# Chunked scan feeding a gated feed-forward: two constant tables filled by VectorE, the first two up-projection units taken by channel half, and one weight product placed behind pair 1's output

## The chip, the cores and the metric

The kernel runs on one core of one Trainium2 chip. The metric is the device time of one execution in microseconds. Each kernel's time is a median over several executions; the profile is of one further execution, whose own time is given beside its span. Engines: PE (TensorE matmul; PEld is its weight load), DVE (VectorE), ACT (ScalarE), POOL (GpSimd), SP (SyncE, which here only issues transfers).

## The reference

Two stages follow each other. The first is a chunked linear recurrence per batch (4) and head (8) over a sequence of 768, with head width D = 32 and state width N = 16; the second multiplies two projections of its result and projects back.

```python
# x (4,8,768,32)  a (4,8,768)  B, C (4,8,768,16)
for c in range(nc):
    cum = cumsum(log a within the chunk)
    L = exp(cum_i - cum_j) * (i >= j)                    # causal
    y_intra = ((C @ B^T) * L) @ x
    y_inter = (C @ state) * exp(cum)
    y = y_intra + y_inter
    state = decay_full * state + sum_j B_j x_j decay_from_j
X = y.transpose(0, 2, 1, 3).reshape(3072, 256)
out = ((X @ w_a) * (X @ w_b)) @ w_out                    # w_a, w_b (256,1536), w_out (1536,256)
```

The output is (3072, 256) in float32.

## The kernel before

The sequence is cut into 6 blocks of 128 tokens. A *pair* is two batches of one block, so there are 12 pairs (pair p is block p // 2). Pairs 0 to 3 go through the feed-forward one pair at a time, in half-precision operands with float32 sums; later blocks go through it a whole block at a time.

For one pair the steps are these. The decays within a block are a product scan on DVE (`scan`, line 227, into `Pr`); B and C are scaled by its quotients (`scale_bc`), turned by PE (`transposes`), and evacuated to `bt` (ACT) and `ct` (DVE). `scores` (line 373) makes C·Bᵀ for all heads in four PSUM banks, `SC[0]` to `SC[3]`; `mask` multiplies each of the four by the table `causal`. Three of the four are done by DVE straight out of PSUM (line 413). The fourth is copied to SBUF by ACT (`tmp`, line 410) and multiplied by POOL (line 411). `scale_x` (line 287, ACT) makes the half-precision `X16` from the loaded `xn`. `pv` multiplies the masked scores with `X16` (line 433), makes the state's terms (line 460), and evacuates the pair's output to `X2T` in two parts, one on ACT (line 492) and one on DVE (line 493). For pair 0 the output is made in two *channel halves* u = 0, 1: `pv_u(0, 0)`, `pv_u(0, 1)`, each followed by two evacuations (`evac0`).

The feed-forward of a pair has 6 *units* k2, each 256 of the 1536 hidden columns. `unit_mm(p, k2, W)` (line 601) is four matmuls of 128x256: two column groups kk, and for each the two channel halves f = 0, 1 that are summed in one PSUM bank. With `Wa` it makes `aps`, which ACT copies to SBUF as `asb` (`evac_a`, line 615); with `Wb` it makes `bps`; DVE multiplies the two into `hk` (`times`, line 622). The output product (line 637) runs over `hk` later.

The order of all work is written out by hand (`manual_schedule`): each engine runs its instructions in the order of the program text, and semaphores carry the dependences between engines. The order around the change is this: pair 0 to its output; `transposes(1)`; units (0,0) and (0,1) with `Wa`; `hr`, `hs`, `hsx` on POOL (three small products, of which `gps` is made); `scores(1)`; the fourth mask of pair 1; unit (0,2) with `Wa`; `factors`; `scale_x(1)`; the three other masks; units (0,0), (0,1), (0,2) with `Wb`; the first `times`; `pv(1)`; the state terms of pair 0; `gps` (line 810) and its copy `G`; the other two `times`; units (1,0), (1,1), (1,2).

PSUM banks for the feed-forward come from `bank(name)` (line 127): four banks, 0 to 3, handed out in the order of the calls by the string `BANKS`. Its first digits are 0 1 2 3 1 0 2 3 1 0 2 3 1 0 1 2 3 0 1; the calls they answer are `fps`, `tb`, `tc`, `py0`, `py1`, three `aps` of pair 0, `fps` of `factors`, three `bps` of pair 0, `gps`, and then `aps` and `bps` of (1,0), of (1,1) and of (1,2). A matmul that starts a new use of a bank waits until the engine that reads the bank's previous content has finished.

Transfers are issued by three engines. SP and ACT issue those of pair 0 at the start. POOL, after it has made its tables `sel`, `ident` and `causal`, issues the rest of pair 1's B and C, the first halves of `Wa` and `Wb`, and pair 1's `xn`; the loads on POOL's queue follow the tables in the order of the text (lines 211 to 216).

Of the kernel before, what the change touches and what calls it, by code (L numbers as in the profile page):

```python
# [28 lines left out]
def kernel(  # L29
# [13 lines left out]
    nc = tc.nc  # L43
# [3 lines left out]
    Q = 128  # L47
# [27 lines left out]
    ident = const.tile([128, 128], f16, name="ident")  # L75
    causal = const.tile([128, 2, Q], f16, name="causal")
# [10 lines left out]
    Wa = [big.tile([128, 2, KC], f16, name=f"Wa{t}") for t in range(2)]  # L87
    Wb = [big.tile([128, 2, KC], f16, name=f"Wb{t}") for t in range(2)]
    Wo = big.tile([128, NK, d_model], f16, name="Wo")
    X2T = big.tile([128, P0, 2, 2, Q], f16, name="X2T")  # L90
# [36 lines left out]
    def bank(name):  # L127
        return psf.tile([128, 512], f32, name=name, tag=f"ff{next(banks)}")
# [58 lines left out]
    load1(nc.sync, 1, 0, 0)  # L187
    nc.sync.dma_start(c32, p32_t.ap())
    nc.vector.memset(warm.bitcast(u32), 0)
    nc.vector.memset(zero, 0.0)  # L190
    nc.gpsimd.memset(sel, 1.0)
    nc.gpsimd.affine_select(
# [5 lines left out]
        pattern=[[-H, 2], [-2 * H, NBP], [-1, H]],  # L198
        channel_multiplier=1,
    )  # L200
    nc.gpsimd.memset(ident, 1.0)
    nc.gpsimd.affine_select(
        out=ident, in_=ident, compare_op=ALU.is_equal, fill=0.0, base=0, pattern=[[-1, 128]], channel_multiplier=1
    )
    nc.gpsimd.memset(causal, 1.0)
    for bt in range(2):
        v = causal[64 * bt : 64 * bt + 64]
        nc.gpsimd.affine_select(  # L208
# [23 lines left out]
    def sel_over_mid(lo, hi, eng):  # L232
        eng.tensor_tensor(
            out=selr[:, lo:hi].rearrange("p k t c -> p k (t c)"),
            in0=sel.rearrange("p t b h -> p (t b h)").unsqueeze(1).broadcast_to((BH, hi - lo, 2 * NBP * H)),
            in1=rmid[:, lo:hi].unsqueeze(2).broadcast_to((BH, hi - lo, 2 * NBP * H)),
            op=ALU.mult,
        )
# [113 lines left out]
    def scores(p):  # L352
        BT, CT = st[p]["BT"], st[p]["CT"]
        st[p]["T1"] = mid.tile([128, H, 2, Q], f16, name="t1", tag="t1")
        for e, bt, m in itertools.product(range(2), range(2), range(4)) if p >= P0 else ():
            rows = slice(32 * m, 32 * m + 32)
            c0 = (e * 2 + bt) * Q
            nc.tensor.matmul(  # L358
                SC[m][:, c0 : c0 + Q],
                BT[rows, e, bt],  # L360
                CT[rows, bt],
                start=True,
                stop=True,
                skip_group_check=True,
                tile_position=(32 * m, 0),
            )
        for e in range(2) if p < P0 else ():
            for r in range(2):
                for m in range(4):
                    for bt in range(2):  # L370
                        rows = slice(32 * m, 32 * m + 32)
                        c0 = (e * 2 + r) * Q
                        nc.tensor.matmul(  # L373
                            SC[m][64 * bt : 64 * bt + 64, c0 : c0 + Q],
                            BT[rows, e, r, bt],
                            CT[rows, bt],
                            start=True,
                            stop=True,
                            skip_group_check=True,
                            tile_position=(32 * m, 64 * bt),  # L380
                        )

    def product(p, m):

        if p >= P0:
            return (
                st[p]["T1"][:, 2 * m : 2 * m + 2].rearrange("p e t q -> p (e t) q"),
                SC[m].rearrange("p (c q) -> p c q", q=Q),
            )
        return (  # L390
            st[p]["T1"][:, 2 * m : 2 * m + 2].rearrange("p e r q -> p e (r q)"),
            SC[m].rearrange("p (e c) -> p e c", e=2),
        )
# [8 lines left out]
    def mask(out_in, by_pool=False, by_token=False):  # L402
        o_, i_ = out_in
        if by_token:
            c_ = causal_q.unsqueeze(1).broadcast_to((128, 4, Q))
        else:
            c_ = causal.rearrange("p r q -> p (r q)").unsqueeze(1).broadcast_to((128, 2, 2 * Q))
        if by_pool:
            tmp = mid.tile([128, *c_.shape[1:]], f32, name="tmp", tag="tmp")
            nc.scalar.copy(tmp, i_)  # L410
            nc.gpsimd.tensor_tensor(out=o_, in0=tmp, in1=c_, op=ALU.mult)  # L411
        else:
            nc.vector.tensor_tensor(out=o_, in0=i_, in1=c_, op=ALU.mult)  # L413
# [182 lines left out]
    def unit_mm(p, k2, W):  # L596
        ps = bank("aps" if W is Wa else "bps")
        for kk in range(2):
            k = 2 * k2 + kk
            for f in range(2):  # L600
                nc.tensor.matmul(  # L601
                    ps[:, kk * 2 * Q : (kk + 1) * 2 * Q],
                    W[k // 6][:, f, k % 6 // 3 * 384 : (k % 6 // 3 + 1) * 384].rearrange("p (c kk) -> p kk c", kk=3)[
                        :, k % 3
                    ],
                    X2T[:, p, :, f],
                    start=(f == 0),
                    stop=(f == 1),
                    skip_group_check=True,
                )  # L610
        return ps

    def evac_a(a_ps, on_dve=False):
        asb = ffh.tile([128, 512], f32, name="asb", tag="asb")
        (nc.vector.tensor_copy if on_dve else nc.scalar.copy)(asb, a_ps)  # L615
        return asb

    def times(p, k2, b_ps, asb):
        s = st[p]
        if "hk" not in s:  # L620
            s["hk"] = ffh.tile([128, NK, 2 * Q], f16, name="hk", tag="hk")
        nc.vector.tensor_tensor(  # L622
            out=s["hk"][:, 2 * k2 : 2 * k2 + 2, :].rearrange("p k q -> p (k q)"), in0=b_ps, in1=asb, op=ALU.mult
        )

    def unit(p, k2, between=None):
        a_ps = unit_mm(p, k2, Wa)
        if between:
            between()
        b_ps = unit_mm(p, k2, Wb)  # L630
        asb = evac_a(a_ps)
        return lambda: times(p, k2, b_ps, asb)
# [26 lines left out]
    def bunit(blk, k):  # L659
        s = st.setdefault(("FF", blk), {})  # L660
        if "hk" not in s:
            s["hk"] = hkb.tile([128, NK, 2 * NBP * Q], f16, name="hkb", tag="hkb")
        ps = []
        for W in (Wa, Wb):
            t_ = bank("aps" if W is Wa else "bps")
            for f in range(2):
                nc.tensor.matmul(  # L667
                    t_,
                    W[k // 6][:, f, k % 6 // 3 * 384 : (k % 6 // 3 + 1) * 384].rearrange("p (c kk) -> p kk c", kk=3)[
                        :, k % 3  # L670
                    ],
                    XB[:, blk - P0 // NBP, f].rearrange("p t j q -> p (t j q)"),
                    start=(f == 0),
                    stop=(f == 1),
                    skip_group_check=True,
                )
            ps.append(t_)
        asb = evac_a(ps[0])
        return lambda: nc.vector.tensor_tensor(out=s["hk"][:, k], in0=ps[1], in1=asb, op=ALU.mult)  # L679
# [93 lines left out]
    scan(5, NBLK)  # L773
    over_mid(1, NBLK)
    sel_over_mid(1, NBLK, nc.vector)
    aps = [unit_mm(0, 0, Wa), unit_mm(0, 1, Wa)]
    asb = [evac_a(aps[0])]
    nc.gpsimd.tensor_tensor(out=hr, in0=Pr[:, 0:NG, Q - 1], in1=rmid[:, 0:NG], op=ALU.mult)
    nc.gpsimd.tensor_tensor(out=hs, in0=hr, in1=Pr[:, 1:NBLK, 63], op=ALU.mult)
    nc.gpsimd.tensor_tensor(  # L780
# [2 lines left out]
        in1=selb.rearrange("p (b g) -> p b g", b=nb),  # L783
        op=ALU.mult,
    )
    scores(1)
    mask(product(1, 3), by_pool=True)
    aps.append(unit_mm(0, 2, Wa))
    asb.append(evac_a(aps[1]))
    asb.append(evac_a(aps[2]))  # L790
# [2 lines left out]
    scale_x(1, nc.scalar)  # L793
    for m in range(3):
        mask(product(1, m))
    bps = [unit_mm(0, k2, Wb) for k2 in range(3)]
    for bt in range(2):
        load1(nc.gpsimd, 2, 1, bt)
    load_wo(0)
# [9 lines left out]
    for c0 in (0, 64):  # L809
# [4 lines left out]
            start=True,  # L814
            stop=True,
            skip_group_check=True,
            tile_position=(0, c0),
        )
    nc.scalar.copy(G.rearrange("p b g -> p (b g)"), gps[:, 0 : nb * NG])
    for k2 in range(1, 3):  # L820
        times(0, k2, bps[k2], asb[k2])
    fb(1)
# [233 lines left out]
```

## Time and profile before

| | us |
|---|---|
| median of 3 runs | 123.72 |
| the runs | 122.92, 124.85, 123.72 |
| the profiled execution | 122.51 |
| span of its profile | 120.8 |
| PE busy | 115.7 (96% of the span) |
| DVE, ACT, POOL busy | 85.2, 72.1, 62.3 |
| first feed-forward matmul, from the span's start | 10.58 |

The profiled execution's own time is 1.71 us longer than its span, and the kernel's time is this sum, not the span alone. Times in the trace count from the span's start. In the chain of waits each piece has its start, its length, its engine, what it writes and its line; in the chain PE's pieces are put by the ends of their matmuls, so a piece starts where the one before it ended. In the timeline each row has start, length, engine, line, operation, output and inputs, count, and in square brackets the idle time ahead of it with what ended it; there a matmul's length holds its whole passage, 0.27 us for one of 128x256, while a new one starts every 0.11 us.

### The profile page before, as it was taken

The page shows a single profiled execution, that of the slowest core. Times are in us where ns is not written, and L with a number is a line of the kernel's source. Part 1 is how long each engine was busy: PE and PEld are TensorE (multiplying, and loading weights), DVE is VectorE, ACT ScalarE, POOL GpSimd, SP SyncE. Part 2 cuts the span into 40 slices and gives each one's busy share as a digit, 9 for nine tenths or more (in the row PEclk, how much of TensorE's full clock was granted, in tenths as well). Part 3 has the DMA queues.
Part 4 walks back from the last instruction along what each step waited for, and adds up shares of the span by engine and source line. Part 5 has one row for each costly group of instructions (what it writes and reads, how often), then busy time and mean ns, then how long its engine had stood idle before and what let it go on. Part 6 is the DMA issues. An engine that isn't in the chain of part 4 may idle for free.

```text
span 120.8 us, 3711 instructions
## 1 busy us (share of the span) xinstructions
PE 115.7 (96%) x1455; PEld 79.4 (66%) x1455; DVE 85.2 (71%) x162; ACT 72.1 (60%) x142; POOL 62.3 (52%) x108
## 2 busy tenths in 40 slices
PE   5889999999999999999999999999999999999990
PEld 2445889888898898644476464766464684555890
DVE  1887888882989898499984999677799445847100
ACT  0466757854965767877668637645646737566220
POOL 7999998972795676299731993138400000000200
PEclk9999999999999999999999999999999999999999
DMA  3999999986969999699998874869501012010032
GB/s 62 171 169 233 173 201 159 215 140 70 100 99 126 128 125 144 111 135 146 71 151 111 173 239 126 91 90 159 180 3 49 0 43 87 0 49 0 20 110 87
DMA packets 66641, 13.73 MB, mean 114 GB/s; under 512 B 61616, under 2 KB 66256, under 8 KB 66624
## 3 DMA queue, kind: packets, MB, share of 16 engines
q1 hardware_dynamic: 62448, 9.40, 50.7%
q0 software_dynamic: 2176, 3.74, 17.0%
q10 hardware_dynamic: 2000, 0.36, 1.6%
q8 instruction: 11, 0.18, 0.7%
q14 instruction: 6, 0.05, 0.1%
HBM read 11.13 MB, written 3.15 MB: 118 GB/s over the span
## 4 chain that ended last, share of the span: by engine, by line
PE 89%; DMA 4%; POOL 3%; issue 0%; ACT 0%; POOLq 0%
PE ops L694 18%; PE aps L667 18%; PE bps L667 17%; PE ops L637 9%; PE aps L601 9%; PE bps L601 9%; DMA Wa<-in_moe_w_a_dram 4%; PE SC L358 2%; PE SC L419 2%; POOL cn L148 1%; PE SC L373 1%; PE SC L433 1%; PE SC L508 1%; POOL bn L148 1%; POOL causal L208 1%; PE SC L460 1%
## 5 line engine op out<-in xcount | busy, mean ns | idle before, releaser
L615 ACT COPY asb<-aps 128x512 f32<-128x512 f32 x72 | 41.8, 586 | 14.1 <-PE aps L667 9.7
L679 DVE TENSOR_TENSOR hkb<-bps,asb 128x512 f16<-128x512 f32 x48 | 32.3, 687 | 12.8 <-ACT asb L615 11.6
L667 PE MATMUL aps<-XB,Wa 128*128 128x512 f16 x96 | 28.6, 379 | 0.0
L667 PE MATMUL bps<-XB,Wb 128*128 128x512 f16 x96 | 28.5, 379 | 0.0
L694 PE MATMUL ops<-Wo,hkb 128*128 128x256 f16 (+1 forms) x204 | 22.5, 267 | 0.0
L694 PEld LDWEIGHTS <-hkb 128*128 128x128 f16 x204 | 18.5, 98 | 3.1
L413 DVE TENSOR_TENSOR t<-SC,causal_q 128x512 f16<-128x512 f32 x27 | 17.1, 681 | 3.3 <-PE SC L358 3.3
L622 DVE TENSOR_TENSOR hk<-bps,asb 128x512 f16<-128x512 f32 x24 | 16.2, 685 | 2.4 <-ACT asb L615 1.2
L667 PEld LDWEIGHTS <-Wb 128*128 128x128 f16 x96 | 9.9, 103 | 10.9
L667 PEld LDWEIGHTS <-Wa 128*128 128x128 f16 x96 | 9.7, 103 | 9.1 <-issue 0.2
L708 POOL DMA_DIRECT2D out_dram<-osb x1 | 0.6, 639 | 27.3 <-ACT osb L706 27.3
L706 ACT ACTIVATE osb<-ops 128x256 f32<-128x256 f32 (+1 forms) x16 | 6.0, 376 | 14.3 <-PE ops L694 14.2
L601 PE MATMUL aps<-X2T,Wa 128*128 128x256 f16 x96 | 14.0, 273 | 0.1
L601 PE MATMUL bps<-X2T,Wb 128*128 128x256 f16 x96 | 13.8, 273 | 0.0
L637 PE MATMUL ops<-Wo,hk 128*128 128x256 f16 x96 | 11.5, 273 | 0.0
L601 PEld LDWEIGHTS <-Wa 128*128 128x128 f16 x96 | 9.5, 104 | 1.1 <-DMA Wa<-in_moe_w_a_dram 0.3
L601 PEld LDWEIGHTS <-Wb 128*128 128x128 f16 x96 | 9.8, 103 | 0.6
L411 POOL TENSOR_TENSOR t<-tmp,causal_q 128x512 f16<-128x512 f32 x5 | 5.8, 1159 | 8.0 <-ACT tmp L410 7.9
L637 PEld LDWEIGHTS <-hk 128*128 128x128 f16 x96 | 8.9, 98 | 1.4
L304 POOL TENSOR_TENSOR bm<-bn,fB 128x256 f16<-128x256 f32 x11 | 7.1, 641 | 4.8 <-DMA bn<-in_B_dram 3.6
L289 POOL TENSOR_SCALAR x<-xn 128x512 f16<-128x512 f32 x6 | 8.9, 1489 | 1.0 <-DMA xn<-in_x_dram 0.7
L296 POOL TENSOR_TENSOR planes<-cn,fC 128x256 f16<-128x256 f32 x8 | 5.0, 621 | 7.9 <-DMA cn<-in_C_dram 7.8
(95 smaller groups left out, 124.0 us busy)
## 6 DMA issues: line engine op xcount, KB each, us to landing
out_dram<-osb SPq DMA_DIRECT2D x22, 128.0 KB, 1.8
xn<-in_x_dram SPq DMA_DIRECT2D x7, 256.0 KB, 4.3
cn<-in_C_dram SPq DMA_DIRECT2D x8, 128.0 KB, 4.1
bn<-in_B_dram SPq DMA_DIRECT2D x8, 128.0 KB, 4.6
Wa<-in_moe_w_a_dram POOLq DMA_DIRECT2D x2, 384.0 KB, 5.9
Wb<-in_moe_w_b_dram POOLq DMA_DIRECT2D x2, 384.0 KB, 7.3
Wo<-in_moe_w_out_dram POOLq DMA_DIRECT2D x2, 384.0 KB, 7.2
xn<-in_x_dram POOLq DMA_DIRECT2D x4, 128.0 KB, 7.2
```

What stands on the lines that cost most here:

```text
L289: eng.tensor_scalar(xo, xi, XS, None, ALU.mult)
L304: eng.tensor_tensor(out=m_, in0=raw, in1=(f[:, blk, :, bp] if factor is None else factor).unsqueeze(3).broadcast_to((128, 2, H, N)), op=AL ...
L411: nc.gpsimd.tensor_tensor(out=o_, in0=tmp, in1=c_, op=ALU.mult)
L413: nc.vector.tensor_tensor(out=o_, in0=i_, in1=c_, op=ALU.mult)
L601: nc.tensor.matmul(ps[:, kk * 2 * Q : (kk + 1) * 2 * Q], W[k // 6][:, f, k % 6 // 3 * 384 : (k % 6 // 3 + 1) * 384].rearrange("p (c kk) -> ...
L615: (nc.vector.tensor_copy if on_dve else nc.scalar.copy)(asb, a_ps)
L622: nc.vector.tensor_tensor(out=s["hk"][:, 2 * k2 : 2 * k2 + 2, :].rearrange("p k q -> p (k q)"), in0=b_ps, in1=asb, op=ALU.mult)
L637: nc.tensor.matmul(o_ps[:, 0:d_model], hk[:, k, bt * Q : (bt + 1) * Q], Wo[:, k, :], start=(k == 0), stop=(k == NK - 1), skip_group_check= ...
L667: nc.tensor.matmul(t_, W[k // 6][:, f, k % 6 // 3 * 384 : (k % 6 // 3 + 1) * 384].rearrange("p (c kk) -> p kk c", kk=3)[:, k % 3], XB[:, b ...
L679: return lambda: nc.vector.tensor_tensor(out=s["hk"][:, k], in0=ps[1], in1=asb, op=ALU.mult)
L694: nc.tensor.matmul(o_ps[:, 0:w], hk[:, k, c * Q : (c + 1) * Q], Wo[:, k, cs], start=(k == 0), stop=(k == NK - 1), skip_group_check=True,)
L706: nc.scalar.activation(out=o_sb[:, 0:w], in_=o_ps[:, 0:w], func=AF.Copy, scale=1.0 / (YS * YS))
```

## The change

Four places are edited.

1. The ones of `ident` and `causal` are written by DVE, between its memsets of `warm` and `zero`, and no longer by POOL. POOL keeps the selections that turn the ones into the two tables.
2. The first two units with `Wa` go through the new `units_mm`, which runs channel half 0 of both units and then channel half 1 of both. The eight matmuls are the same, and the accumulation flag that clears a bank is set on the bank's first matmul alone.
3. `scores(1)` and the fourth mask of pair 1 stand ahead of `hr`, `hs` and `hsx`, so that POOL's product with the mask comes before these three.
4. The third `Wb` product of pair 0 (unit (0,2)) stands behind `pv(1)`, `gps` and the copy `G`. Its call of `bank` thereby comes after that of `gps`; the string `BANKS` is not changed.

```diff
     nc.vector.memset(warm.bitcast(u32), 0)
+    nc.vector.memset(ident, 1.0)
+    nc.vector.memset(causal, 1.0)
     nc.vector.memset(zero, 0.0)
...
-    nc.gpsimd.memset(ident, 1.0)
     nc.gpsimd.affine_select(
         out=ident, in_=ident, compare_op=ALU.is_equal, fill=0.0, base=0, pattern=[[-1, 128]], channel_multiplier=1
     )
-    nc.gpsimd.memset(causal, 1.0)
...
+    def units_mm(p, ks, W, order):
+        pss = {k2: bank("aps" if W is Wa else "bps") for k2 in ks}
+        for k2, f in order:
+            for kk in range(2):
+                k = 2 * k2 + kk
+                nc.tensor.matmul(
+                    pss[k2][:, kk * 2 * Q : (kk + 1) * 2 * Q],
+                    W[k // 6][:, f, k % 6 // 3 * 384 : (k % 6 // 3 + 1) * 384].rearrange("p (c kk) -> p kk c", kk=3)[
+                        :, k % 3
+                    ],
+                    X2T[:, p, :, f],
+                    start=(f == 0 and kk == 0),
+                    stop=(f == 1),
+                    skip_group_check=True,
+                )
+        return [pss[k2] for k2 in ks]
...
-    aps = [unit_mm(0, 0, Wa), unit_mm(0, 1, Wa)]
+    aps = units_mm(0, range(2), Wa, ((0, 0), (1, 0), (0, 1), (1, 1)))
     asb = [evac_a(aps[0])]
+    scores(1)
+    mask(product(1, 3), by_pool=True)
     nc.gpsimd.tensor_tensor(out=hr, in0=Pr[:, 0:NG, Q - 1], in1=rmid[:, 0:NG], op=ALU.mult)
...
-    scores(1)
-    mask(product(1, 3), by_pool=True)
     aps.append(unit_mm(0, 2, Wa))
...
-    bps = [unit_mm(0, k2, Wb) for k2 in range(3)]
+    bps = [unit_mm(0, k2, Wb) for k2 in range(2)]
...
     nc.scalar.copy(G.rearrange("p b g -> p (b g)"), gps[:, 0 : nb * NG])
+    bps.append(unit_mm(0, 2, Wb))
     for k2 in range(1, 3):
         times(0, k2, bps[k2], asb[k2])
```

## The prediction

> **What bounds the kernel now.** I read the page's shares first, then the chain of waits in order of time, then the timelines of POOL, ACT, DVE and PE from 0 to 21 us, and last the transfers' shares in stretches of half a microsecond.
>
> ```profile
> PE 115.7 (96%) x1455; PEld 79.4 (66%) x1455; DVE 85.2 (71%) x162; ACT 72.1 (60%) x142; POOL 62.3 (52%) x108
> ...
> PE 89%; DMA 4%; POOL 3%; issue 0%; ACT 0%; POOLq 0%
> ```
>
> PE carries 89% of the chain that ended last; only its beginning belongs to others. The chain in time shows where:
>
> ```profile
> 2.93 0.83 POOL bn L148
> 3.75 1.35 POOL cn L148 x2
> 5.11 5.43 DMA Wa<-in_moe_w_a_dram
> 10.58 1.06 PE aps L601 x8
> ...
> 13.38 1.43 PE bps L601 x12
> 14.80 0.35 PE SC L433 x32
> 15.33 0.28 PE SC L460 x24
> 15.62 0.22 PE gps L810 x4
> 15.84 0.55 PE aps L601 x4
> 16.39 0.44 PE bps L601 x4
> ```
>
> POOL makes tables until 2.88, issues three loads, then Wa's; Wa lands at 10.54 and PE starts the feed-forward at 10.58. From there on PE's pieces follow each other to 118.0, with gaps of 0.2 us at most (15.15 to 15.33). So whatever PE gains or loses once before 17 us stays to the end. What decides is where (1,0)'s `bps` ends: 16.39 + 0.44 = 16.83.
>
> **Part 1, the ones.** POOL's rows:
>
> ```profile
> 1.18 0.20 POOL L201 MEMSET ident<- 128x128 f16 x1
> 1.45 0.29 POOL L202 TENSOR_SCALAR_AFFINE_SELECT ident<-ident 128x128 f16<-128x128 f16 x1
> 1.69 0.31 POOL L205 MEMSET causal<- 128x256 f16 x1
> 2.07 0.86 POOL L208 TENSOR_SCALAR_AFFINE_SELECT causal<-causal 64x256 f16<-64x256 f16 x2
> ```
>
> DVE wrote 256 columns of `warm` in 0.27 us and 128 of `zero` in 0.165, the second 0.23 after the first. So `ident` is ready at about 1.15 + 0.17 = 1.32 and `causal` at 1.28 + 0.27 = 1.55. POOL's `ident` selection can start at 1.37 (DVE's `bm` ends at 5.52 and PE follows at 5.57, so 0.05 for a semaphore), its next instruction 0.24 later (1.45 to 1.69), so `causal`'s selection at about 1.62, not 2.07: 0.45 earlier. Bounds: 0 if POOL waits as long for DVE as it worked itself, 0.51 by the two durations. All POOL issues up to `xn` move by 0.45. On DVE it costs nothing: `zero` ends at about 1.7, and the scan waits for its input until 3.07.
>
> Do the loads land 0.45 earlier? The 16 transfer engines:
>
> ```profile
> 5.00:5.50 0.50, 0.24 (x2) 0.00 (x0) 0.47 (x3) 0.00 (x0) 0.50 (x2) 1.00 0.89 199
> 5.50:6.00 0.50, 0.42 (x5) 0.27 (x6) 0.35 (x2) 0.10 (x1) 0.50 (x2) 1.00 1.34 306
> ```
>
> The last two columns are their share and GB/s. Until 5.5 us the share is 0.74 to 0.94 (from 2.5 on) and POOL's queue moves almost nothing outside 4.5 to 5.0; there is room. From 5.5 to 12 it is 1.07 to 1.51, and POOL's loads land one behind another: Wa 10.54, Wb 12.83, the two `xn` about 13.35 and 13.97. Work moved into the room before 5.5 brings them all forward, the rest only changes places. Bounds 0 and 0.45; I take 0.30, nearer the upper end, since from 4.0 to 5.5 the shares (about 0.9) leave a sixth to two fifths of what later stretches carry (1.07 to 1.51).
>
> The Trainium skill, DMA: Bandwidth & Descriptors, "Issuing engines are not separate DMA queues", says that transfers of all queues share the same 16 engines and that concurrent issue saves only the issuer's time. The landings one behind another agree. By it alone the gain would be 0 and the sum below +1.00.
>
> At the front PE then starts at about 10.28. The transposes of pair 1 allow it: POOL's line 411 waits for ACT's `tmp` (7.87), starts at 7.92, not 8.05, so the transposes move from 10.04 to 9.91 and are through by 10.2.
>
> **Part 2, channel half first.** X2T's second half is ready at 9.96 + 0.29 = 10.25. From 10.28 the old order would have needed it at 10.39, the new one at 10.72: nothing either way. `aps` of (0,0) is full after six matmuls, at 10.28 + 0.27 + 5 x 0.11 = 11.1; ACT is on `bt` until about 11.2 (0.84 from 10.35). Without that cover it would cost 0.22 on ACT.
>
> **Part 3, the mask first on POOL.** The product starts at about 12.65, when POOL's issues end, and ends at 13.8, not 14.71. `hsx` ends at 13.8 + 0.8 = 14.6, not 13.58; `gps` needs it at about 15.3. The next loads on POOL start when both are done, as now. Nothing, except that the mask no longer holds line 433; if `hsx` lost its cover of 0.7, PE would wait for the excess.
>
> **Part 4, the third product.** Now line 433 waits for `X16`:
>
> ```profile
> 13.56 0.33 ACT L273 COPY fC<-fps 128x160 f32<-128x160 f32 x1
> 14.03 0.63 ACT L287 ACTIVATE x<-xn 128x512 f16<-128x512 f32 x1
> ...
> 15.60 1.28 DVE L622 TENSOR_TENSOR hk<-bps,asb 128x512 f16<-128x512 f32 x2
> ```
>
> ACT is free at 13.89 and starts line 287 at 14.03, just after `xn` landed; PE's weight load of line 433 waited 0.2 us for it, 14.53 to 14.73. So pair 1's output hangs on `xn`, not on PE. The third product's four matmuls (0.44) lay in that wait. Taken out, PE has its eight matmuls done at 14.80 - 0.44 - 0.30 = 14.06 and stands idle until 14.80 - 0.30 = 14.50; behind `gps` the 0.44 comes back as time of its own. **+0.44.**
>
> Then the bank. `gps` now gets bank 3 and the third product bank 1, which (1,0)'s `bps` uses next. Before, that wait was for ACT's copy of `gps` (15.89 + 0.17 = 16.06, in time for 16.28). Now it is for DVE's `times` of the third product, and only (1,0)'s four `aps` matmuls lie between. From the product's last end: 0.10 until DVE starts (`bps` end 19.89 + 0.44 = 20.33, DVE at 20.43), 0.69 for the product, 0.05 to PE, 0.27 for the first matmul to pass: 1.11. Without the wait it would have ended after 0.55. **+0.56** of standing PE, with all later units queued behind it. DVE is free in time: its previous product ends 1.49 after line 433's start, the third product 1.04 + 0.55 = 1.59. Bounds: 0 (if the cover held) to 0.66 (0.10 for a semaphore, the larger of the two rows).
>
> **Sum:** +0.44 + 0.56 - 0.30 = +0.70, between +0.55 and +1.00 as `xn` moves. On the profiled execution's 122.51 (span 120.8 and 1.71 around it) this is 123.21. The median shown, 123.72, is 1.21 above that execution; the middle of the four known executions is (122.92 + 123.72) / 2 = 123.32. I add to that: **124.0 us**.
>
> **The rivals.** *Nothing lands earlier*: the shares above 1 decide alone; PE then waits for `X16` until 14.73 as now. +1.00: 124.3. For it: landings in a row. Against: the idle room before 5.5. *The bank wait is covered*: if the 0.56 were hidden, +0.14: 123.5. Against: 0.69 of DVE against 0.44 of matmuls. *Faster, the lead carries through*: if PE's earlier start at 10.28 met neither wait, 123.32 - 0.30 = 123.0. It decides from `xn` landing by about 13.3, so that `X16` is there at 14.06, and from DVE freeing the bank within 0.44. For it: the first feed-forward matmul does hang on Wa alone. Against: `xn` would have to move 0.67, more than POOL's whole 0.45. *Slower, the clock*: PE stands for 0.44 + 0.56 = 1.0 us within 14 to 17.3. At the start its matmuls of 512 columns come 0.43 apart (weight loads at 1.65 to 3.78) and later 0.22, so half rate exists. If idling brought that back for 4 us, 2.0 us of work would be lost: 123.32 + 0.70 + 2.0 = 126.0. Against: 5.0 to 8.5 has 0.66 us of idle PE and the rate held. It decides somewhere between 0.66 and 1.0 of idle in 3.5.
>
> The Trainium skill, TensorE: Matmul & The Clock Gate, "Why this matters for your kernels", asks for an idle gap of about 3 us before the clock falls; by it this rival is empty. No run here has such a gap; the clock column reads 1.00 throughout the early stretches.
>
> **How the numbers follow.** Chances: forecast 0.68, nothing earlier 0.15, bank covered 0.07, lead carries 0.04, clock 0.04, others 0.02. The cases differ by less than the executions of before do among themselves (122.51 to 124.85), so the range takes that spread: low 122.51 + 0.14, about 122.7; high 124.85 + 0.70, about 125.5. Over 2% either way (2.5 us, about what a measurement of this kernel can tell from no change) is reached by the clock alone, and by the spread with little: faster 0.02, within 0.93, slower 0.05.
>
> **What would show it.** Right: POOL's first issue near 2.43; PE's first `aps` near 10.28; line 287 at 13.6 to 13.9, with PE idle ahead of line 433; PE idle about half a microsecond ahead of (1,0)'s `bps`, released by DVE's `times`; that `bps` ending at 17.4 to 17.8, not 16.83, and the rest of the chain shifted as much. Wrong: line 287 before 13.5; (1,0)'s `bps` following its `aps` without a gap; a later stretch of PE that gives the loss back; matmuls of 128x512 more than 0.3 apart after 14 us.

## The result, and the profile after

| | before | after |
|---|---|---|
| median, us (22 runs each) | 123.30 | 123.78 |
| ratio after / before, 95% interval | | 1.0059 (1.0042 to 1.0076) |
| the profiled execution: time, span | 122.51, 120.8 | 123.78, 122.1 |
| PE busy in the profile, us | 115.7 | 116.5 |
| (1,0)'s `bps` complete, from the span's start | 16.83 | 18.08 |

The change makes the kernel slower by 0.6%: 0.0059 x 123.30 = 0.73 us (0.52 to 0.94). The ratio is worked out from the executions in the faster of two states alone and is not the quotient of the two medians, which lie 0.48 us apart. The two profiled executions lie 1.27 us apart; the one of before was among the fastest of its kernel, the one of after in the middle of its own. Nearly all of these 1.27 us are there when (1,0)'s `bps` is complete: 18.08 - 16.83 = 1.25.

The chain of waits of the changed kernel in order of time (start, length, engine, what it writes, line):

```profile
2.55 0.83 POOL bn L148
3.37 1.37 POOL cn L148 x2
4.74 0.73 POOL Wa L165
5.47 0.73 POOL Wb L165
6.21 0.66 POOL xn L148
6.86 7.31 DMA xn<-in_x_dram
...
14.26 0.64 ACT x L287
14.90 0.04 issue
14.94 0.42 PE SC L433 x32
...
15.86 0.22 PE gps L827 x4
16.08 0.57 PE bps L601 x4
...
16.74 0.70 DVE hk L639
17.44 0.04 issue
17.48 0.60 PE bps L601 x4
18.08 0.44 PE aps L601 x4
```

Two pieces that do not belong to PE are new in it. The load of `xn` and ACT's `X16` now release pair 1's output (line 433), where before the chain was PE's own from 10.58 on. And DVE's product (`hk`, line 639) stands between the third `Wb` product, complete at 16.64, and (1,0)'s `bps`. The timeline of PE in the changed kernel shows the second wait from the other side; the bracket is the idle time and what ended it:

```profile
16.01 0.62 PE L601 MATMUL bps<-X2T,Wb 128*128 128x256 f16 x4
16.47 0.60 PE L601 MATMUL aps<-X2T,Wa 128*128 128x256 f16 x4
17.48 0.60 PE L601 MATMUL bps<-X2T,Wb 128*128 128x256 f16 x4 [0.41 <-DVE hk L639]
```

The front did not become earlier. POOL's and DVE's timelines of the changed kernel:

```profile
1.40 0.29 POOL L203 TENSOR_SCALAR_AFFINE_SELECT ident<-ident 128x128 f16<-128x128 f16 x1 [0.17 <-DVE ident L190]
1.67 0.87 POOL L208 TENSOR_SCALAR_AFFINE_SELECT causal<-causal 64x256 f16<-64x256 f16 x2
2.50 0.88 POOL L148 DMA_DIRECT2D bn<-in_B_dram  x1
```

```profile
5.77 0.42 DVE L304 TENSOR_TENSOR cm<-cn,fps 128x256 f16<-128x256 f32 x1 [0.16 <-DMA cn<-in_C_dram]
```

POOL issues its first load at 2.50, not 2.88, as the ones by DVE should make it. But pair 0's `cm`, which started at 5.44 before, now waits for pair 0's C and starts at 5.77, and all of pair 0 follows 0.33 us later: the transposes of pair 1 start at 10.39 (before 10.04), the first `aps` at 10.71 (before 10.58).

### The profile page after: what moved, and what is told of

Its sections match the earlier page's. It is cut to its first block, busy times and chain, and to the rows that moved or that the text cites. A ratio compares the mean times of both kernels' runs of the same rounds, so it can differ in the third digit from the quotient of the medians.

```text
span 122.1 us, 3712 instructions
## 1 busy us (share of the span) xinstructions
PE 116.5 (95%) x1455; PEld 79.6 (65%) x1455; DVE 86.0 (70%) x164; ACT 72.2 (59%) x142; POOL 61.7 (51%) x106
## 4 chain that ended last, share of the span: by engine, by line
PE 85%; DMA 6%; POOL 4%; DVE 1%; ACT 1%; issue 0%; DVEq 0%; ACTq 0%
PE ops L711 18%; PE aps L684 17%; PE bps L684 17%; PE ops L654 9%; PE bps L601 8%; PE aps L601 7%; DMA xn<-in_x_dram 6%; PE SC L358 2%; PE SC L419 2%; POOL cn L148 1%; PE SC L433 1%; PE SC L508 1%; POOL bn L148 1%; POOL causal L208 1%; POOL Wa L165 1%; POOL Wb L165 1%
## 5 line engine op out<-in xcount | busy, mean ns | idle before, releaser
L696 DVE TENSOR_TENSOR hkb<-bps,asb 128x512 f16<-128x512 f32 x48 | 32.3, 688 | 12.7 <-ACT asb L632 11.6
L684 PEld LDWEIGHTS <-Wa 128*128 128x128 f16 x96 | 9.7, 103 | 9.1 <-issue 0.2
L601 PE MATMUL aps<-X2T,Wa 128*128 128x256 f16 x88 | 12.9, 273 | 0.0
L601 PEld LDWEIGHTS <-Wa 128*128 128x128 f16 x88 | 8.8, 103 | 0.7
```

The lines of the kernel that those rows point to most:

```text
L601: nc.tensor.matmul(ps[:, kk * 2 * Q : (kk + 1) * 2 * Q], W[k // 6][:, f, k % 6 // 3 * 384 : (k % 6 // 3 + 1) * 384].rearrange("p (c kk) -> ...
L684: nc.tensor.matmul(t_, W[k // 6][:, f, k % 6 // 3 * 384 : (k % 6 // 3 + 1) * 384].rearrange("p (c kk) -> p kk c", kk=3)[:, k % 3], XB[:, b ...
```

## The experiments

Ten kernels, each timed in five rounds beside the kernel before. Two theories were open after the result. The prediction's: the bank wait costs 0.56, the product's new place 0.44, and the earlier loads give 0.30 back. The rival that the trace of after suggests: the earlier loads give nothing, because they only change places with pair 0's. The microseconds below are the ratio less 1, times the median of the kernel before in that set (123.03, 123.07 and 122.79).

| kernel | ratio to before | 95% interval | us |
|---|---|---|---|
| part 1 alone (e_ones) | 1.0018 | 0.9989 to 1.0047 | +0.22 |
| parts 2 and 3 (p23) | 0.9989 | 0.9963 to 1.0015 | -0.14 |
| parts 1 to 3 (c_nothird) | 1.0013 | 0.9985 to 1.0040 | +0.16 |
| parts 2 to 4 (d_noones) | 1.0076 | 1.0045 to 1.0107 | +0.94 |
| part 4 alone (b_third) | 1.0069 | 1.0046 to 1.0091 | +0.85 |
| part 4 alone, banks exchanged (b_third_bank) | 1.0016 | 0.9986 to 1.0046 | +0.20 |
| all parts, banks exchanged (a_bank) | 1.0034 | 1.0004 to 1.0064 | +0.42 |
| before, POOL's loads issued later (e_late) | 1.0068 | 1.0034 to 1.0102 | +0.83 |
| xn between two quarters of Wb (k_split) | 1.0024 | 0.9998 to 1.0051 | +0.30 |
| Wa as POOL's second load (wa_first) | 1.0157 | 1.0089 to 1.0224 | +1.93 |

**The bank, in the changed kernel** (a_bank).

```diff
-    "0123102310231012301230123012031230123013201320130213021302130213021320312031203102132013"
+    "0123102310213012301230123012031230123013201320130213021302130213021320312031203102132013"
```

> The changed kernel with two digits of the bank string exchanged, so that gps has bank 1 and the third Wb product bank 3. Theory of the prediction: (1,0)'s bps then waits for ACT's short copy of gps, not for DVE's product; the gap of PE ahead of it goes and the time falls by 0.56 us against the changed kernel, to 0.0 to +0.2 us of the kernel before. Rival (the bank wait is not what counts, the order of the third product alone is): no change against the changed kernel, still +0.5 to +0.7 over the kernel before.

Its chain of waits has no DVE between the third product and (1,0)'s `bps`:

```profile
6.86 7.58 DMA xn<-in_x_dram
...
15.21 0.42 PE SC L433 x32
...
15.75 0.33 issue
16.08 0.27 PE SC L460 x20
16.35 0.22 PE gps L827 x4
16.57 0.55 PE bps L601 x4
17.12 0.44 PE aps L601 x4
17.56 0.44 PE bps L601 x4
```

From the third product's end (17.12) to that of (1,0)'s `bps` it takes 0.88 us; in the changed kernel it took 16.64 to 18.08, 1.44. The difference, 0.56, is the term of the prediction. In time it is less clear: +0.42 (0.05 to 0.79) over before against +0.73, with intervals that overlap; the 0.0 to +0.2 that was expected lies at the low end of its interval. In this execution (1,0)'s `bps` is complete at 18.00, only 0.08 before that of the changed kernel: `xn` landed 0.26 later (14.44, not 14.18), and the piece "issue" at line 460 is 0.33, not 0.10.

**Part 4 alone** (b_third), and the same with the banks exchanged (b_third_bank).

```diff
-    bps = [unit_mm(0, k2, Wb) for k2 in range(3)]
+    bps = [unit_mm(0, k2, Wb) for k2 in range(2)]
...
     nc.scalar.copy(G.rearrange("p b g -> p (b g)"), gps[:, 0 : nb * NG])
+    bps.append(unit_mm(0, 2, Wb))
```

> The kernel before with the third Wb product moved behind pair 1's output and nothing else. Theory of the prediction: +0.44 (the four matmuls leave the wait for X16) +0.56 (bank wait) = +1.0 us over the kernel before. Rival (the bank wait is covered): +0.44 us.

> The kernel before with the third Wb product behind pair 1's output and the two bank digits exchanged, so that gps has bank 1 and the product bank 3. Theory of the prediction: the bank wait's 0.56 goes and 0.44 of the product itself stays: +0.3 to +0.5 us over the kernel before, where the same without the exchange had +0.85. Rival (the bank counts for nothing): +0.85 again.

+0.85 us with the bank wait and +0.20 without, so the wait is worth about 0.65 us; the two intervals just touch (1.0046). What is left for the product's place, +0.20 (-0.17 to +0.57), is under half of the 0.44, which the interval still holds. The chain of the second kernel shows how it can be less:

```profile
12.73 0.98 ACT asb L615 x2
13.71 0.17 ACT fC L273
13.88 0.04 issue
13.92 0.64 ACT x L287
14.56 0.04 issue
14.60 0.51 PE SC L433 x29
...
15.62 0.55 PE bps L601 x4
16.17 0.44 PE aps L601 x4
16.61 0.44 PE bps L601 x4
```

In this execution `xn` was there in time: ACT starts `X16` at 13.92, right behind its copy of `fC`, and line 433 starts at 14.60, earlier than the 14.73 of before, because PE has four matmuls less ahead of it. So pair 1's output does not always hang on `xn`: PE and `X16` are ready within a few tenths of each other, and which is late differs between profiled executions with the same loads (ACT starts `X16` at 13.74 to 14.46 in the kernels with the ones on POOL, in the table below).

**The ones** (e_ones: part 1 alone; d_noones: all but part 1; c_nothird: all but part 4).

```diff
+    nc.vector.memset(ident, 1.0)
+    nc.vector.memset(causal, 1.0)
     nc.vector.memset(zero, 0.0)
...
-    nc.gpsimd.memset(ident, 1.0)
...
-    nc.gpsimd.memset(causal, 1.0)
```

(d_noones is the changed kernel with these lines as they were; c_nothird is the changed kernel with the third product as it was.)

> The kernel before with the ones of ident and causal written by DVE and nothing else (part 1 alone). Theory of the prediction: POOL issues 0.4 us earlier, xn lands 0.30 earlier, -0.30 us against the kernel before. Theory after the first four runs: the transfer engines are full from 5.5 us on, the loads only change places; POOL issues at 2.5, but Wa and xn land no earlier (xn 14.0 to 14.5) and pair 0's cm and x on DVE and ACT start 0.1 to 0.3 later; 0.0 to +0.2 us.

> The changed kernel with the ones of ident and causal written by POOL again: parts 2 to 4. Theory of the prediction: loses the 0.30 us of the earlier loads, so +1.0 us over the kernel before. Rival (the earlier issue brings nothing): the same time as the changed kernel, +0.5 to +0.7 us over the kernel before; if it delays pair 0's C, even less.

> The changed kernel with the third Wb product back in its old place: parts 1 to 3 alone. Theory of the prediction: xn lands 0.30 us earlier and PE's start moves with it, -0.30 us against the kernel before. Rival (the earlier issue only changes places among the loads, and pair 0's C lands later for it, as the changed kernel's trace has it): 0 to +0.2 us over the kernel before.

Part 1 alone is not faster: +0.22 us, with an interval that allows -0.14 at best and excludes -0.30. With parts 2 and 3 it is +0.16. d_noones doesn't decide; its interval (+0.55 to +1.3 us) holds both expectations. The traces are clearer than the times. The chain of e_ones:

```profile
6.87 7.62 DMA xn<-in_x_dram
...
14.56 0.64 ACT x L287
...
15.25 0.50 PE SC L433 x32
```

| from the profiles (us) | POOL's ones: before, p23, b_third, b_third_bank, d_noones | DVE's ones: after, a_bank, c_nothird, e_ones |
|---|---|---|
| POOL's first issue | 2.87 to 2.88 | 2.49 to 2.50 |
| Wa, from issue to landing | 5.3 to 5.5 | 5.8 to 6.3 |
| xn, from issue to landing (median of two) | 6.5 to 7.0 | 7.3 to 7.7 |
| ACT starts pair 1's X16 | 13.74 to 14.46 | 14.26 to 14.57 |
| DVE starts pair 0's cm | 5.43 to 5.53 | 5.55 to 5.77 |
| pair 0's two 32 KB loads of C (SP, ACT), from issue to landing | 2.7 to 3.0 (d_noones: not recorded) | 3.1 to 3.5 |

The issue is 0.38 earlier, and Wa takes about 0.65 longer and `xn` 0.8 (middle of each group); they land no earlier, on the whole later. One load did gain: the first of pair 1's C lands at 7.0 to 7.3, not at 7.9 to 8.4, but nothing waits for it, since pair 1's `cm` starts at 9.1 or later in all of them.

**Later issue** (e_late). The opposite step tells whether the place of the loads counts at all:

```diff
+    for _ in range(2):
+        nc.gpsimd.memset(maskbd, 0.0)
     load1(nc.gpsimd, 1, 0, 1)
```

> The kernel before with two more memsets on POOL (of maskbd, which is written again later) ahead of its first load, so that all of POOL's loads are issued about 0.5 us later. If the landing follows the issue (theory of the prediction, its upper end): Wa lands near 11.0, xn near 14.5, +0.4 to +0.5 us over the kernel before. If the engines' work decides (the landing does not follow the issue): Wa stays at 10.5 to 10.6, xn at 13.7 to 14.4, within 0.2 us of the kernel before; if the loads collide with pair 0's, pair 0's cm on DVE starts no later than 5.45.

```profile
4.50 1.37 POOL cn L148 x2
5.86 0.73 POOL Wa L165
6.60 0.73 POOL Wb L165
7.33 0.66 POOL xn L148
7.99 7.01 DMA xn<-in_x_dram
...
15.08 0.64 ACT x L289
```

The first load is issued at 3.62, 0.74 later than before. Wa takes 5.4 us as before and lands 0.7 later (first `aps` at 11.29, before 10.58); `xn` takes 7.0 and lands at 14.99, 1.0 later. So these landings follow a later issue, while 0.38 of earlier issue brings them nothing: there is a knee, and the kernel before stood near it.

The time rises by 0.83 us (0.42 to 1.25), but that is not the price of the loads alone, because the two memsets hold POOL itself back as well. Its product for pair 0 starts at 8.80 (before 8.05) and its `bm` of pair 1 at 9.92 (before 9.17), and PE waits for both:

```profile
10.01 0.30 PE L435 MATMUL py<-t,x 64*32 64x128 f16 x14 [0.18 <-POOL t L413]
10.78 0.28 PE L328 MATMUL SC<-ident,bm 128*128 128x128 f16 x2 [0.30 <-POOL bm L306]
```

How the 0.83 is shared between late loads and a late POOL was not tested. The sign that was expected of a collision with pair 0's loads, `cm` no later than 5.45, did not come: `cm` starts at 5.52, as in the kernels with the ones on POOL. The loads themselves tell more: pair 0's two small loads of C, which SP and ACT issue, take 2.8 us here, 2.7 to 3.0 in the other kernels with the ones on POOL, and 3.1 to 3.5 with the earlier issue. That speaks for a collision; which transfers hold up which was not measured.

**Parts 2 and 3** (p23: the changed kernel without parts 1 and 4).

> The kernel before with parts 2 and 3 (channel half first, mask first on POOL), without the ones on DVE and with the third Wb product in its old place. Theory of the prediction and after the first four runs: 0.0 us, both lie beside other work (within 0.2 us). Rival (they carry a part of the loss, hsx ending 1 us later or aps of (0,0) being full later): +0.2 us or more.

-0.14 us (-0.46 to +0.18): no cost, and no gain that can be told from none. It has the lowest ratio of all, but it cannot be told from the kernel before. Its profiled execution also shows that the front is not all that lets single executions differ: (1,0)'s `bps` is complete at 16.84, level with before, and yet the execution is 0.46 us longer (122.97); PE stands for 0.27 us between 30 and 40 us, and its chain runs over later loads of C and B from 21.5 to 32.3.

**Two tries at a faster one.** k_split is p23 with the first half of Wb as two tiles:

```diff
-    load_w(0)
...
+    nc.gpsimd.dma_start(Wa[0], wa0[:, :, 0:KC])
+    nc.gpsimd.dma_start(Wb0[0], wb0[:, :, 0 : KC // 2])
     for bt in range(2):
         load1(nc.gpsimd, 1, 2, bt)
+    nc.gpsimd.dma_start(Wb0[1], wb0[:, :, KC // 2 : KC])
...
-    factors(1, NBLK, fps)
+    factors_mm(1, NBLK, fps)
     scale_x(1, nc.scalar)
+    nc.scalar.copy(flat(fC, 1, NBLK), fps[:, 0 : (NBLK - 1) * 2 * NBP * H])
```

> The kernel before with parts 2 and 3, and the first half of Wb loaded in two quarters of 192 KB with pair 1's xn between them; ACT makes pair 1's X16 ahead of the copy of fC. Theory (pair 1's output hangs on xn, and xn on the bytes ahead of it): xn lands about 1 us earlier, near 13.1, PE no longer waits for X16 at line 433, and the time falls by what that wait cost, 0.1 to 0.5 us below the kernel before. Rival (PE itself was the limit there, or the split loads are slower or the second quarter is late): 0.0 us or slower.

Its chain of waits:

```profile
5.11 6.71 DMA Wa<-in_moe_w_a_dram
...
11.87 1.06 PE aps L628 x8
```

Wa, issued at the same time as before and ahead of all that changed, took 6.71 us in place of 5.43, and PE started 1.3 us late. `xn`, with half of Wb's bytes no longer ahead of it, landed no earlier: at about 13.6 and 14.0 (before 13.35 and 13.97). This looks as if the loads of one queue were not served strictly one after the other, and as if what is queued behind a load could delay it. It is one execution, though, and among the longer ones of its kernel (123.77, median 123.31); the cause is not shown. +0.30 us (-0.02 to +0.63), not a gain.

wa_first is p23 with Wa ahead of pair 1's two loads of C.

```diff
     load1(nc.gpsimd, 1, 0, 1)
...
+    nc.gpsimd.dma_start(Wa[0], wa0)
     load1(nc.gpsimd, 1, 1, 0)
     load1(nc.gpsimd, 1, 1, 1)
-    load_w(0)
+    nc.gpsimd.dma_start(Wb[0], wb0)
```

> Parts 2 and 3, and Wa's first half issued as the second of POOL's loads, ahead of pair 1's two loads of C. Theory: Wa is there before the transposes of pair 1, PE starts the first units at about 10.3 and the time falls by up to 0.2 us below the kernel before, if xn lands no later. Rival: Wa's large packets take the engines from pair 0's loads (pair 0's cm later than 5.45, its x later than 7.8), and the time is that of the kernel before or more.

+1.93 us (1.09 to 2.75), from only six runs between 123.59 and 126.50; the profiled one is the fastest of them, and its (1,0)'s `bps` is complete at 17.90, 1.07 later than in before. Pair 1's C, issued right behind Wa, landed at 5.17 + 5.72 = 10.89, and a load of pair 1's B, which SP issues at 3.8, took 6.4 us (before 4.6). So `cm` and `bm` of pair 1, its transposes and its scores were late by more than a microsecond. Pair 0's `cm` and `x` moved only to 5.53 and 7.96 (p23 5.43 and 7.76): most of the price was paid by pair 1, not by pair 0 as the rival had it.

## Why the prediction was right, and where it was not

The forecast was +0.70 us, 124.0 us; measured are +0.73 (0.52 to 0.94) and 123.78. The base was right: the middle of four executions, 123.32, against a median of 123.30 over 22. The sum was nearer than its terms.

- **The bank wait, +0.56:** right. In the trace of after it takes 17.48 + 0.27 - 16.64 = 1.11 us from the third product's end to the first matmul's end of (1,0)'s `bps`, which is the 1.11 that was added up; exchanging the two banks takes the wait away, and 0.65 us of the time of part 4. DVE was free only just in time: in b_third its previous product ends at 16.69 and the third one starts at 16.75. (The upper bound, 0.66, should be 0.61: with 0.10 for a semaphore only the 0.05 to PE changes.)
- **The product's place, +0.44:** the mechanism held, the size only where `xn` is late. In the profiled execution of after it is whole: PE was done with the `bps` ahead of line 433 at 14.51 and stood until 14.94. Over many executions it measured +0.20 (-0.17 to +0.57, so 0.44 is not excluded). The step that failed is "pair 1's output hangs on `xn`, not on PE". It rested on the 0.2 us ahead of line 433's weight loads, which was read as a wait for `X16`. The line of before, and the same loads in k_split (there line 443):

```profile
14.73 0.24 PEld L433 LDWEIGHTS <-x 64*32 64x32 f16 x32 [0.20 <-ACT x L287]
...
16.02 0.24 PEld L443 LDWEIGHTS <-x 64*32 64x32 f16 x32 [0.20 <-issue]
```

  In k_split `X16` had been done since 15.50, half a microsecond, and the 0.20 stands there all the same, as it does in wa_first (0.3 us after `X16`) and in p23 (0.21, 0.25 us after it). So in the execution that was read, PE and `X16` (done at 14.66) were ready together, and with four matmuls less PE can use an early `xn`.
- **The earlier loads, -0.30:** wrong, in its sign for this profiled execution. The step was "work moved into the room before 5.5 brings them all forward". POOL's issue did move (0.38, forecast 0.45), and neither Wa nor Wb nor `xn` landed earlier for it. From after's trace +0.21 has to stand there (line 433 at 14.94, before 14.73), and with 0.44 and 0.56 that makes 1.21 of the 1.25 at (1,0)'s `bps`. The bound taken from the rows, 0 to 0.45, was open downwards: that earlier loads could hold up pair 0's was not priced. The Trainium skill, DMA: Bandwidth & Descriptors, "Issuing engines are not separate DMA queues" (concurrent issue saves only the issuer's time), was the better guide for the earlier issue; of a later issue it says nothing, and in e_late the landings follow the issue.
- **Parts 2 and 3 at nothing:** right, -0.14 (-0.46 to +0.18).
- **The rivals.** *Nothing lands earlier* had the right mechanism of the loads; its price, +1.00, was worked out from the profiled execution, where +1.27 was measured, and lies above the interval of the ratio (0.52 to 0.94). *The bank covered* and *the lead carries through* did not happen: both waits are in the chain. *The clock* did not move either. The stretches of the changed kernel in which PE stood (engines' busy time, then granted clock, transfer share, GB/s):

```profile
14.50:15.00 0.50, 0.07 (x9) 0.06 (x16) 0.30 (x1) 0.39 (x1) 0.36 (x2) 1.00 1.09 187
17.00:17.50 0.50, 0.09 (x2) 0.02 (x1) 0.50 (x2) 0.40 (x1) 0.50 (x2) 1.00 1.24 268
```

  PE was busy for 0.07 and 0.09 us of these half microseconds. The clock column stays at 1.00, but it reads 1.00 from 2.0 to 4.0 us of before too, where the prediction counts half rate, so it cannot decide. What decides is that the groups of four matmuls behind the gaps take 0.44 us each in the chain of after (from 18.08 on), as in before: the rate held. The Trainium skill, TensorE: Matmul & The Clock Gate, "Why this matters for your kernels", agrees as far as these gaps go; none of about 3 us was run.

Where the two wrong terms point to different sides (-0.30 was too good, +0.44 too bad), they cancelled over many executions, so that the sum came out this close is in part luck. The measured parts add up to 0.22 - 0.14 + 0.20 + 0.65 = 0.93, against 0.73 measured for all of them; with intervals of about 0.35 on each, no interaction between them is shown.

## What to carry to other kernels

When work moves past a call that takes a buffer from a rotation, list who had and who gets each buffer: here two digits of a string cost more than all the rest of the change, and the diff didn't show them. A wait that one execution shows as just covered is a coin toss over many; take out work that hides under it only when both sides have slack. Before a load is issued earlier, see whether its flight grows by as much; issuing it later is a cheap test of whether it was waiting for its issue at all, as long as nothing else on that engine is moved with it.

## What the runs showed of the hardware that was not expected

- The landing of the same loads against their issue is a knee, not a line: issued 0.38 earlier, Wa and `xn` flew about 0.65 and 0.8 longer; issued 0.74 later, they landed 0.7 and 1.0 later.
- A large load on one queue goes with a slower load on another: with Wa issued at 3.75, not 5.11, a load of pair 1's B that SP issues at 3.8 took 6.4 us, where it took 4.4 to 5.0 in all the other kernels. That a load can be delayed by what stands behind it in its own queue is suggested by one execution alone: Wa's flight was 6.71, not 5.43, when the 384 KB of Wb behind it were cut into two loads with `xn` between them.
- The pieces "issue" in PE's chain between the small matmuls of line 460 (PE waits for nothing that the profile shows) were 0.09 us before, 0.10 in after, 0.33 in a_bank, 0.41 in e_late and 0.44 in d_noones. Where they come from was not tried; they are a part of what lets single executions differ.
